# Routing attention and feed-forward: batch 2's feed-forward by seven products too, behind the attention

## The chip, the cores and the metric

The kernel runs on one core of one Trainium2 chip. The metric is the device time of a run in microseconds; three runs of the kernel before gave 957.65, 957.71 and 958.09 us, so the median is 957.71 us. PE is TensorE (matmuls), PEld its weight loads, DVE is VectorE, ACT is ScalarE, POOL is GpSimd, SP is SyncE, which only issues DMAs here.

## The reference

Inputs: `q`, `k`, `v` of 4 batches x 8 heads x 768 tokens x 64, and 16 centroids per head; `w_in` 512 x 2048, `w_out` 2048 x 512, `alpha` 2048, both weight matrices in double precision.

```python
q_assign = np.argmax(np.einsum('bhsd,hcd->bhsc', q_n, c_n), axis=-1)
k_assign = np.argmax(np.einsum('bhsd,hcd->bhsc', k_n, c_n), axis=-1)
mask = q_assign[:, :, :, None] == k_assign[:, :, None, :]
scores = np.where(mask, scale * np.matmul(q, k.transpose(0, 1, 3, 2)), -1000000000.0)
attn = softmax(scores)
x = np.matmul(attn, v)                 # then (B,H,S,D) -> (B*S, H*D) = 3072 x 512
h = x @ w_in
g = np.maximum(h, 0.0) + alpha * np.minimum(h, 0.0)
out = g @ w_out                        # 3072 x 512
```

A query attends only to keys of the same cluster. The feed-forward of one batch is 768 x 512 by 512 x 2048 and 768 x 2048 by 2048 x 512, in fp32.

## The kernel before, in words

**Attention.** Two heads make a pair; there are 16 pairs, four to a batch. Pairs 0 to 9 are taken in halves of 384 queries, each half in three steps: scores for all six chunks of 128 keys, exp on ScalarE, a mask on VectorE (`mask`, L795; from pair 4 on), sums for the denominators (`add_up`, `turn`, `rows_sums`), and the weighing of v on TensorE (`weigh`, L878). Pairs 10 to 15 are sorted by cluster first, so that each chunk of keys needs only two or three chunks of queries; a sorted pair is taken whole, in three steps (`add_near`, L819; `weigh_near`, L921; `normalise_near`, L937). The sort (`order_features` to `order_clusters`, L562 to L643) computes ranks on VectorE; then GpSimd scatters tokens into `scratch` by 24 indirect DMAs (`order_scatter`, L655) from two `stage` tiles that SP loads (`order_stage`, L645), and SP loads the sorted pair (`order_load`, L669). `ORDERS` (L1330) holds the step at which each sorted pair's sort begins. After a sorted pair, 12 indirect DMAs put the result back in token order (`put_back`, L970), SP fetches it (`fetch_back`, L977), and VectorE turns it into x (`turn_back`, L989).

The order of all work is written out by hand: one loop over 78 steps, each of five slots; a counter, `tick()`, runs with the slots, and `later(n, piece)` puts a piece n ticks on. In the first step of a half or pair (L1467 to L1494) come: scores of three chunks, the inverse of the prior pair's denominators (`invert`, L860), its weighing, three masks, its normalising, and scores of the other three chunks. The totals that `invert` reads are a TensorE matmul (`total`, L850), issued a few slots after the row sums, in the prior pair's own last slots.

**Feed-forward.** Regular feed-forward of half a batch (`ffn_pieces`, L1010) is 28 *pieces*: 16 hidden pieces (four matmuls of 384 columns, a copy on ScalarE, the slope on VectorE) and 12 finals (four matmuls of 512 columns; two finals fill one bank). They lie in a queue, `ffn`, and the loop takes some in each slot, so that TensorE has work while the attention waits. When a half of a batch's attention is done, `feed_block` (L1387) puts its 28 pieces in the queue; they are spread evenly over the slots of the next block of steps, and `kept` (L1396) says how many are left over at the block's end. Blocks, named here by letters, with their start and end in the profiled execution:

| block | steps | attention in it | pieces taken, before | us |
|---|---|---|---|---|
| A | 24 to 35 | pairs 4 to 7, first halves | 30 | 196.6 to 324.9 |
| B | 36 to 47 | pairs 4 to 7, second halves | 28 | 324.9 to 452.5 |
| C | 48 to 59 | sorted 10 and 11; 8 and 9, first halves | 26 | 452.5 to 571.5 |
| D | 60 to 65 | 8 and 9, second halves | 22 | 571.5 to 652.9 |
| E | 66 to 77 | sorted 12 to 15 | 24 | 652.9 to 761.9 |

What is left, 12 pieces, covers the last pair's way back (`while due`, L1536: two ticks for each piece). Then `last_pieces` (L1103) does batch 3 by seven products for eight (Strassen's scheme in Winograd's form): the x of the batch is split in four quarters, `w_in` and `w_out` likewise, sums of quarters are formed on VectorE (`sum_x` L1092, `w_in_sums` L1080, `g_sums` L1179, `w_out_sums` L1186), and seven products of quarters are added up in PSUM and on VectorE. First eight inner tiles x of `hidden` (L1197; six pieces of two matmuls of 384 columns and one late one), then three token tiles of `final` (L1253; seven products of eight matmuls of 256 columns). Sums of g are formed per inner tile, for all tokens at once, beside the hidden products.

Of the kernel before, what the change touches and what calls it, by code (L numbers as in the profile page):

```python
# [23 lines left out]
def kernel(  # L24
# [629 lines left out]

    def order_scatter(n, i, x):  # L655
        h, part = divmod(i, PARTS)
# [12 lines left out]
    def order_load(n):  # L669
        whole = scratch.pop(n)[0]  # L670
# [266 lines left out]
    def normalise_near(n):  # L937
# [20 lines left out]
        later(starts[1] + 2 + (HJ if dense else NJ), lambda: fetch_back(n, whole))  # L958
# [18 lines left out]
    def fetch_back(n, whole):  # L977

        b, hp = pairs[n]
        raw = inp.tile([P, 2, NJ, D], FP32, name="qk").rearrange("p h j d -> p (h j d)")  # L980
# [8 lines left out]
        def turn_back():  # L989
            for half in range(2):  # L990
                nc.vector.transpose(out=x_tile(b, half)[:, hp, :],
                                    in_=raw[:, half * HS:(half + 1) * HS])
        later(4 if n == NP - 1 else 9, turn_back)

# [12 lines left out]

    unfinished = [False]
# [61 lines left out]
    KH, NQ, HC = NCH // 2, NF // 2, DM // 2  # L1070
# [7 lines left out]
    by_pair, x_sums = {}, []  # L1078
# [13 lines left out]
    def sum_x(which):  # L1092
        x0, x1 = (xTs[B - 1, half] for half in range(2))
        if not x_sums:
            x_sums.extend(vpool.tile([P, 2, NJ, D], FP32, name="vt").rearrange(
                "p h j d -> p (h j d)").rearrange("p (c q) -> p c q", c=KH)
                for _ in range(3))
        T1, T2, T4 = x_sums
        B11, B21, B12, B22 = (x0[:, 0:KH], x0[:, KH:NCH], x1[:, 0:KH], x1[:, KH:NCH])
        for to, x, y in ((T1, B12, B11), (T2, B22, T1), (B12, B22, B12), (T4, B21, T2))[which]:  # L1100
            nc.vector.tensor_tensor(out=to, in0=x, in1=y, op=ALU.subtract)

    def last_pieces():  # L1103
        b = B - 1
        rows = out[b * S:(b + 1) * S, :].rearrange("(j p) n -> p j n", p=P)
        g, ys, s4, order = {}, [], [], []

        def places():

            whole = [e.rearrange("p h q -> p (h q)") for e in e_tiles]  # L1110
            whole += [inp.tile([P, 2, NJ, D], FP32, name="qk").rearrange(
                "p h j d -> p (h j d)") for _ in range(4)]
            single = [gpool.tile([P, HS], FP32, name="gT") for _ in range(NF // 2)]
            for x in range(NQ):
                for f in (x, NQ + x):
                    if whole:
                        t = whole.pop(0)
                        g[f] = [t[:, h * HS:(h + 1) * HS] for h in range(2)], t
                    else:
                        g[f] = [single.pop(0) for _ in range(2)], None  # L1120
            assert not whole
            s4.extend(single)
            more = [accp.tile([P, 2 * NX, Q], FP32, name="acc").rearrange("p x i -> p (x i)")
                    for _ in range(2)]
            more.append(vpool.tile([P, 2, NJ, D], FP32, name="vt").rearrange(
                "p h j d -> p (h j d)"))
            s4.extend(t[:, h * HS:(h + 1) * HS] for t in more for h in range(2))
            assert len(s4) >= NQ
# [13 lines left out]
        def slopes(f):  # L1142
            halves, both = g[f]
            for t in halves if both is None else [both]:
                nc.vector.scalar_tensor_tensor(out=t, in0=t, scalar=alpha[:, f:f + 1], in1=t,
                                               op0=ALU.mult, op1=ALU.max)
# [10 lines left out]
        def g_sum(x, m):  # L1157

            if m == "S4":
                return s4[x]  # L1160
            t = by_pair[x // 2].rearrange("p (x m q) -> p x m q", x=2, m=2)
            return t[:, x % 2, ("S1", "S2").index(m)]

        def g_form(m, x, t):
            r = slice(t * P, (t + 1) * P)
            if m in ("11", "12", "22", "S3"):
                f, half = {"11": (x, 0), "12": (NQ + x, 0), "22": (NQ + x, 1), "S3": (x, 1)}[m]
                return g[f][0][half][:, r]
            return g_sum(x, m)[:, r]
# [8 lines left out]

        def g_sums(x):  # L1179
            (t0, t1), (z0, z1) = g[x][0], g[NQ + x][0]  # L1180
            S1, S2, S4 = (g_sum(x, m) for m in ("S1", "S2", "S4"))
            for to, p, q, op in ((S1, t1, z1, ALU.add), (S2, S1, t0, ALU.subtract),
                                 (t1, t0, t1, ALU.subtract), (S4, z0, S2, ALU.subtract)):
                nc.vector.tensor_tensor(out=to, in0=p, in1=q, op=op)
# [12 lines left out]
        def hidden(x):  # L1197
# [3 lines left out]
            def product(to, m, rhs, start):  # L1201
                if start:
                    bank[to] = new_bank(to)[:, 0:HS]
                for cc in range(KH):
                    nc.tensor.matmul(out=bank[to], lhsT=w_in_form(m, x, cc),  # L1205
                                     rhs=rhs[:, cc, :], start=start and cc == 0,
# [3 lines left out]
            def x_of(half, kh):  # L1210
                return xTs[b, half][:, kh * KH:(kh + 1) * KH]

            def g_of(f, half):
                return g[f][0][half]

            def p1():
                if not g:
                    places()
                copy(g_of(f1, 0), product("a", "11", x_of(0, 0), True))

            def p5():
                copy(g_of(f2, 1), product("e", "S1", x_sums[0], True))
# [535 lines left out]
```

## Time and profile before

| | |
|---|---|
| median of three runs | 957.71 us |
| the profiled execution's own time | 958.22 us |
| its span, first to last instruction | 956.3 us |
| granted TensorE clock, mean | 0.997 |
| attention beside regular feed-forward, blocks A to E | 565.3 us |
| from there to the first of batch 3's products | 41.1 us |
| batch 3: hidden products, second products and the end | 73.8 and 79.5 us |

A profile shows how long each engine was busy and what it waited for. Idle time of an engine that is not the bottleneck costs nothing. In the tables by stretch the number in brackets is a count of instructions. TensorE records each fp32 matmul twice.

### The profile page before, as it was taken

The numbers are of one execution on the slowest core, as the hardware profiler recorded it, in microseconds if no ns is written. First come the engines' busy times: TensorE is split into PE (matmuls) and PEld (weight loads), VectorE is DVE, ScalarE is ACT, GpSimd is POOL, SyncE is SP. The second block draws the span as 40 slices with busy tenths as digits, with TensorE's granted clock in tenths as the row PEclk, the third lists the DMA queues.
The fourth block names the chain that finished last, engine by engine and source line by source line (L and its number), as shares of the span: only waits on it lengthen the run. The fifth ranks groups of instructions, "written<-read, shape, count | busy, mean of one in ns | idle before, by whom it ended". The sixth has DMA issues, their size and how long they took to land.

```text
span 956.3 us, 11347 instructions
## 1 busy us (share of the span) xinstructions
PE 929.1 (97%) x3995; PEld 496.8 (52%) x3995; DVE 669.4 (70%) x1235; ACT 251.5 (26%) x462; POOL 297.8 (31%) x333
## 2 busy tenths in 40 slices
PE   8999999999999999989999999999999999999997
PEld 5534444445454454444544545545455454556886
DVE  5797698799588697788894975556888536598100
ACT  5664544323032121220222212222122110221000
POOL 1433222210006365423277774640055440000000
PEclk9999999999999999999999999999999999999998
DMA  7433666047004444432842236441041011000000
GB/s 293 140 112 108 143 124 135 17 89 164 1 0 110 121 121 85 83 64 66 138 97 61 57 83 117 96 85 34 23 88 33 21 34 52 1 0 1 23 23 25
DMA packets 209664, 73.35 MB, mean 77 GB/s; under 512 B 194288, under 2 KB 198080, under 8 KB 209600
## 3 DMA queue, kind: packets, MB, share of 16 engines
q1 hardware_dynamic: 201840, 60.35, 28.5%
q0 software_dynamic: 6912, 11.81, 3.7%
q8 instruction: 33, 0.54, 0.2%
q10 hardware_dynamic: 848, 0.39, 0.2%
q14 instruction: 31, 0.25, 0.1%
HBM read 49.89 MB, written 22.28 MB: 75 GB/s over the span
## 4 chain that ended last, share of the span: by engine, by line
PE 77%; DVE 12%; issue 8%; POOL 2%; ACT 1%; DMA 0%; DVEq 0%; POOLq 0%; ACTq 0%
PE fps L1045 23%; PE fps L1027 17%; PE vps L901 7%; PE sps L765 6%; PE sps L1261 4%; PE sps L1205 4%; PE fps L765 2%; PE vps L1261 2%; PE vps L1205 2%; DVE acc L816 1%; PE fps L1261 1%; PE fps L1205 1%; DVE gT L1019 1%; DVE more L806 1%; PE vps L934 1%
## 5 line engine op out<-in xcount | busy, mean ns | idle before, releaser
L1027 PE MATMUL fps<-xT,w_in_sb 128*128 128x384 f32 x768 | 259.2, 491 | 0.0
L1045 PE MATMUL fps<-w_out_sb,gT 128*128 128x512 f32 x576 | 255.7, 596 | 1.1 <-DVE gT L1019 1.1
L663 POOL DMA_INDIRECT scratch<-stage,off x144 | 155.0, 1076 | 222.7 <-DMA stage<-in_v_dram 95.6
L1027 PEld LDWEIGHTS fps<-xT,w_in_sb 128*128 128x128 f32 x768 | 142.4, 190 | 103.6 <-issue 3.9
L1045 PEld LDWEIGHTS fps<-w_out_sb,gT 128*128 128x128 f32 x576 | 107.0, 190 | 129.0 <-issue 119.6
L972 POOL DMA_INDIRECT back<-rows,found x72 | 74.3, 1032 | 113.4 <-ACT rows L967 94.0
L1033 ACT COPY gT<-fps 128x384 f32<-128x384 f32 x96 | 46.0, 479 | 230.3 <-PE fps L1027 230.3
L1019 DVE SCALAR_TENSOR_TENSOR gT<-gT,alpha 128x384 f32<-128x384 f32 x96 | 61.5, 649 | 49.7 <-ACT gT L1033 49.5
L765 PE MATMUL sps<-qkT 64*128 64x384 f32 (+1 forms) x480 | 89.2, 490 | 0.0
L806 DVE SCALAR_TENSOR_TENSOR more<-aq,key,more 128x384 f32<-128x384 bf16 (+1 forms) x120 | 65.0, 598 | 19.3 <-ACT more L786 15.7
L786 ACT ACTIVATE E<-sps 128x768 f32<-128x768 f32 (+1 forms) x78 | 58.3, 796 | 62.5 <-PE sps L774 38.4
L765 PEld LDWEIGHTS sps<-qkT 64*128 64x128 f32 x480 | 42.8, 186 | 41.4 <-issue 14.4
L806 DVE SCALAR_TENSOR_TENSOR E<-aq,key,E 128x384 f32<-128x384 bf16 (+1 forms) x96 | 51.6, 595 | 17.7 <-ACT E L786 15.4
L901 PE MATMUL vps<-E,vt 128*64 128x384 f32 x316 | 58.6, 495 | 1.5 <-DVE xT L1003 1.5
L271 POOL TENSOR_TENSOR w_in_sb<-w_in_sb,power 128x512 f32<-128x512 f32 x16 | 26.9, 1683 | 67.8 <-DVE w_in_sb L268 67.8
L816 DVE TENSOR_TENSOR acc<-acc,E 128x768 f32<-128x768 f32 x37 | 35.2, 952 | 14.7 <-ACT E L786 13.6
L786 ACT ACTIVATE more<-sps 128x768 f32<-128x768 f32 (+1 forms) x42 | 31.4, 783 | 40.6 <-PE sps L765 40.0
L271 POOL TENSOR_TENSOR w_out_sb<-w_out_sb,power 128x512 f32<-128x512 f32 x16 | 22.6, 1412 | 56.0 <-DVE w_out_sb L268 56.0
L1051 ACT COPY y<-fps 128x512 f32<-128x512 f32 x18 | 10.6, 586 | 105.7 <-PE fps L1045 105.7
L1053 DVE TENSOR_TENSOR y<-y,fps 128x512 f32<-128x512 f32 x24 | 16.4, 683 | 29.8 <-PE fps L1045 29.8
L901 PEld LDWEIGHTS vps<-E,vt 128*64 128x64 f32 x316 | 20.1, 136 | 29.3 <-issue 26.8
L765 PE MATMUL fps<-qkT 64*128 64x384 f32 x144 | 31.8, 509 | 0.0
(281 smaller groups left out, 1106.1 us busy)
## 6 DMA issues: line engine op xcount, KB each, us to landing
raw<-in_moe_w_in_dram SPq DMA_DIRECT2D x16, 512.0 KB, 5.8
raw<-in_moe_w_out_dram SPq DMA_DIRECT2D x16, 512.0 KB, 4.3
out_dram<-y SPq DMA_DIRECT2D x21, 256.0 KB, 2.1
qk<-in_q_dram SPq DMA_DIRECT2D x48, 96.0 KB, 4.0
qk<-in_k_dram SPq DMA_DIRECT2D x48, 96.0 KB, 3.7
qk<-scratch SPq DMA_DIRECT2D x48, 96.0 KB, 3.4
w_in_kept<-w_in_sb SPq DMA_DIRECT2D x8, 512.0 KB, 4.7
vt<-in_v_dram SPq DMA_DIRECT2D x10, 384.0 KB, 4.3
```

The costliest lines, as they stand in the source:

```text
L271: nc.gpsimd.tensor_tensor(out=dst, in0=dst, in1=power[0].bitcast(FP32), op=ALU.mult)
L663: nc.gpsimd.indirect_dma_start(out=scratch[n][1][h * NX + xx], out_offset=bass.IndirectOffsetOnAxis(ap=ranks[n][:, xx, h:h + 1], axis=0), ...
L765: nc.tensor.matmul(out=bank(ps, h, m), lhsT=qkT[r:r + D, S + c * P:S + (c + 1) * P], rhs=qkT[r:r + D, tokens], start=True, stop=not early_ ...
L786: nc.scalar.activation(out=E[:, :, 0:m], in_=ps[:, :, 0:m], func=AF.Exp, scale=SCALE)
L806: nc.vector.scalar_tensor_tensor(out=e, in0=of, scalar=keys[n][:, NJ + c, h:h + 1], in1=e, op0=ALU.is_equal, op1=ALU.mult)
L901: nc.tensor.matmul(out=po[r:r + D, 0:HS], lhsT=vts[n][:, h, c, :], rhs=e[:, h, :], start=(c == 0), stop=(c == NJ - 1))
L972: nc.gpsimd.indirect_dma_start(out=to[i], out_offset=bass.IndirectOffsetOnAxis(ap=place[:, h, j:j + 1], axis=0), in_=rows[j // HJ][:, j % ...
L1019: nc.vector.scalar_tensor_tensor(out=gs[f], in0=gs[f], scalar=alpha[:, f:f + 1], in1=gs[f], op0=ALU.mult, op1=ALU.max)
L1027: nc.tensor.matmul(out=ps[:, 0:HS], lhsT=w_in_sb[:, c, f * P:(f + 1) * P], rhs=xTs[b, half][:, c, :], start=(c == 0), stop=(c == NCH - 1))
L1045: nc.tensor.matmul(out=ps[:, 0:DM], lhsT=gs[f][:, i * P:(i + 1) * P], rhs=w_out_sb[:, f, :], start=on and f == f0, stop=off and f == f0 + ...
L1205: nc.tensor.matmul(out=bank[to], lhsT=w_in_form(m, x, cc), rhs=rhs[:, cc, :], start=start and cc == 0, stop=cc == KH - 1, skip_group_check ...
L1261: nc.tensor.matmul(out=bank[to], lhsT=g_form(m, x, t), rhs=w_out_form(n, x), start=start and x == 0, stop=x == NQ - 1, skip_group_check=no ...
```

## The change

Regular feed-forward is now made only for batches 0 and 1. Batches 2 and 3 both go by seven products, after the attention: first the hidden products of batch 2, then of batch 3, then the second products of batch 2's three token tiles and batch 3's three. The regular pieces that are left are spread anew (`kept`). To find room, sums of g are formed per token tile: after each product of `final` that used a sum, the same sum for the next token tile is formed in its place. Batch 3's x lies in four E tiles, and its pairs 12 to 14 are fetched back after the last step. The matmul of totals moves from the pair's last slots to the next pair's first step, behind its first scores. Two scatters may go in a slot of the first step. Sorts begin at other steps, and the features of a sort come one step after the load instead of two.

```diff
-        later(starts[1] + 2 + (HJ if dense else NJ), lambda: fetch_back(n, whole))
+        backs[n] = whole
+        if pairs[n][0] < B - 1:
+            later(starts[1] + 2 + NJ, lambda: fetch_back(n))
+        elif dense:
+            for i in range(NCH):
+                later((1, 3, 5, starts[1] + 2 + HJ)[i],
+                      lambda i=i: fetch_back(NP - NCH + i))
...
+    def x_quarter(b, half, kh):
+
+        if b < B - 1:
+            return x_tile(b, half)[:, kh * KH:(kh + 1) * KH]
+        return e_tiles[2 * half + kh]
...
+    def sum_x(b):
+        B11, B21, B12, B22 = (x_quarter(b, half, kh) for half in range(2) for kh in range(2))
...
+        for c in range(KH):
+            for to, x, y in ((T1[c], B12[:, c], B11[:, c]), (T2[c], B22[:, c], T1[c]),
+                             (T4[c], B21[:, c], T2[c])):
+                nc.vector.tensor_tensor(out=to, in0=x, in1=y, op=ALU.subtract)
+        nc.vector.tensor_tensor(out=B12, in0=B22, in1=B12, op=ALU.subtract)
...
+        def g_sums(b, t, m):
             r = slice(t * P, (t + 1) * P)
+            for x in range(NQ):
+                t0, t1, z0, z1 = (g_tile(b, k, x)[:, r] for k in ("11", "21", "12", "22"))
+                p, q, op = {"S1": (t1, z1, ALU.add), "S2": (g_sum("S1", x), t0, ALU.subtract),
+                            "S3": (t0, t1, ALU.subtract),
+                            "S4": (z0, g_sum("S2", x), ALU.subtract)}[m]
+                nc.vector.tensor_tensor(out=g_sum(m, x), in0=p, in1=q, op=op)
...
                 late.append(p4)
-                if x % 2 == 0 and x:
-                    g_sums(x - 2)
-                    w_out_sums(x - 2)
-                    if x // 2 + 1 < NQ // 2:
+                if b == B - 2:
+                    if x in (2, 4):
                         w_in_sums(x // 2 + 1)
                 elif x > 1:
-                    g_sums(x - 2)
                     w_out_sums(x - 2)
+                    if x == NQ - 1:
+                        g_sums(B - 2, 0, "S1")
...
+                if m in ("S1", "S2", "S3", "S4") and k + 1 < 2 * HJ:
+                    g_sums(B - 2 + (k + 1) // HJ, (k + 1) % HJ, m)
...
-            def store(i, c0, c1):
-                nc.sync.dma_start(out=rows[:, i, c0:c1], in_=ys[i][:, c0:c1])
+            def store(i, *halves):
+                for c0 in halves:
+                    nc.sync.dma_start(out=rows[b][:, i * HJ + t, c0:c0 + HC],
+                                      in_=(y1 if i else y0)(c0))
...
         pieces = []
-        for x in range(NQ):
-            pieces += hidden(x)
-        pieces.append(room_for_y)
-        for t in range(HJ):
-            pieces += final(t)
+        for b in (B - 2, B - 1):
+            for x in range(NQ):
+                pieces += hidden(b, x)
+        pieces.append(second_products)
+        for k in range(2 * HJ):
+            pieces += final(k)
         return pieces
...
-    ORDERS = [26, 30, 34, 38, 41, 51]
+    ORDERS = [26, 29, 35, 38, 41, 50]
...
-                at(t + 2, 2 + i, lambda n=n, i=i: order_features(n, i))
-            at(t + 3, FIRST + 1, lambda n=n: order_sims(n))
+                at(t + 1, FIRST + i, lambda n=n, i=i: order_features(n, i))
+            at(t + 2, 2, lambda n=n: order_sims(n))
...
-            for i, p in ((5, 0), (7, 1)):
-                ffn[i] = lambda piece=ffn[i], p=p: (piece(), w_in_sums(p))
+            sums = [lambda: sum_x(WHOLE - 1), lambda: w_in_sums(0), lambda: w_in_sums(1)]
+            for i, also in enumerate(sums):
+                ffn[i] = lambda piece=ffn[i], also=also: (piece(), also())
             ffn.extend(last_pieces())
-            return
-        ffn.extend(ffn_pieces(*feeds[u]))
+        elif feeds[u][0] < WHOLE - 1:
+            ffn.extend(ffn_pieces(*feeds[u]))
...
-        return {NS: 12, begun_at[-2]: 8, begun_at[-3]: 2}.get(block_end(u), 0)
+        return dict(zip(begun_at[-5:], (7, 12, 19, 14, 6))).get(block_end(u), 0)
...
                 score(n, half, range(0, NJ // 2), alone=NJ // 2 - 1)
+            total(prior[0])
             tick()
...
-                todo += [lambda: None] * 4 + [lambda n=n: total(n)]
+                todo += [lambda: None] * 5
...
-            while sorting:
+            room = 1 + (s == 0)
+            while sorting and room:
                 scatters, piece = sorting.popleft()
                 piece()
-                if scatters:
-                    break
+                room -= scatters
...
+    late_pieces = len(ffn) - kept(NS - 1)
     while due:
         tick()
-        if due:
-            tick()
-        feed(1)
-    sum_x(slice(0, 4))
+        feed(1 if unfinished[0] or len(ffn) > late_pieces else 3)
+    sum_x(B - 1)
```

## The prediction

> **What bounds the kernel now.** I read the page first, then the busy time of each engine by stretch, then the chain of waits, then the instructions of VectorE and GpSimd in order of time. "Block" and "piece" are meant as in the section on the kernel.
>
> ```profile
> span 956.3 us, 11347 instructions
> ...
> PE 929.1 (97%) x3995; PEld 496.8 (52%) x3995; DVE 669.4 (70%) x1235; ACT 251.5 (26%) x462; POOL 297.8 (31%) x333
> ...
> PE   8999999999999999989999999999999999999997
> ...
> DVE  5797698799588697788894975556888536598100
> ```
>
> TensorE is busy 97% of the span with no weak slice but the ends: it sets the time, and only 27 us could be won by filling its gaps. VectorE has 70% over all, but eight or nine tenths in many slices of the attention. The busy time by block (columns: stretch, its length, PE, PEld, DVE, ACT, POOL, granted clock, DMA share, GB/s):
>
> ```profile
> 196.60:324.90 128.30, 126.24 (x469) 61.18 (x468) 98.27 (x178) 27.94 (x53) 22.70 (x31) 1.00 0.33 75
> 324.90:452.50 127.60, 123.05 (x473) 60.62 (x472) 106.44 (x191) 28.25 (x53) 57.42 (x61) 1.00 0.41 93
> 452.50:571.50 119.00, 114.96 (x475) 58.79 (x474) 95.09 (x174) 28.93 (x57) 75.86 (x79) 1.00 0.42 87
> 571.50:652.90 81.40, 81.40 (x287) 41.50 (x286) 45.41 (x76) 17.39 (x34) 38.80 (x44) 1.00 0.51 99
> 652.90:761.90 109.00, 107.14 (x443) 55.41 (x442) 84.52 (x151) 27.32 (x55) 32.80 (x33) 1.00 0.17 35
> 761.90:803.00 41.10, 41.10 (x144) 21.32 (x144) 18.73 (x39) 4.11 (x9) 15.54 (x16) 1.00 0.18 40
> 803.00:876.80 73.80, 72.85 (x228) 42.51 (x227) 53.26 (x108) 14.86 (x31) 0.00 (x0) 1.00 0.02 8
> 876.80:956.30 79.50, 72.57 (x337) 63.53 (x335) 13.42 (x32) 4.96 (x13) 0.00 (x0) 0.97 0.06 21
> ```
>
> The first five rows are blocks A to E (565.3 us). TensorE stands still for 12.5 us of them, VectorE for 135.6 us. In A to E TensorE is full only because feed-forward pieces are laid between the attention's steps. The last two rows are batch 3's feed-forward by seven products: VectorE has room there.
>
> What a column costs on TensorE, from the chain that ended last (start, us, what; every fp32 matmul leaves two records):
>
> ```profile
> 304.19 17.16 PE fps L1045 x40
> 586.89 12.90 PE fps L1027 x40
> ...
> 824.03 2.58 PE sps L1205 x8
> ...
> 894.11 10.36 PE sps L1261 x48
> ```
>
> Per record 429 ns (512 columns), 322 (384), 322 (384, products), 216 (256, products): 0.84 ns a column everywhere. So seven eighths of the columns is seven eighths of the time.
>
> [...] In the blocks above the granted clock is 1.00 and no gap of TensorE is over 1.9 us[...]. [...] The trace has 558 ns for 384 and 422 for 256[...] (the nearest row, a 128x128 add at L545, took 0.29 us).
>
> **The change part by part.**
>
> 1. *TensorE's saving.* A batch of regular feed-forward is 2 x (64 matmuls of 384 columns at 0.645 + 48 of 512 at 0.858) = 165 us; by seven products 112 x 0.645 + 168 x 0.432 = 145 us. Saved: 20.5 us, certain.
>
> 2. *Fewer pieces beside the attention.* From the feeding rule with the new `kept`: 23 pieces in A (30 before), 23 in B (28), 22 in C (26 before, 21 plus one to finish a pair of finals), 4 in D (22), 8 in E (24), and 6 after. What the attention itself takes is block minus pieces: L1027 and L1045 have, in A, 43.42 us for 16 hidden pieces and 49.20 for 14 finals, so 2.71 and 3.51 us each; L1019 has 0.61 us of VectorE per hidden piece, L1053 0.68 per second final. Own times of the attention: PE 33.6, 37.4, 36.3, 16.1, 31.7; DVE 85.1, 94.8, 84.2, 35.9, 75.1.
>    - A: 15 hidden, 8 final: PE 33.6 + 40.7 + 28.1 = 102.4; DVE 85.1 + 9.2 + 2.0 = 96.3
>    - B: 11 and 12: PE 37.4 + 29.8 + 42.1 = 109.3; DVE 94.8 + 6.7 + 2.0 = 103.5
>    - C: 14 and 8: PE 36.3 + 37.9 + 28.1 = 102.3; DVE 84.2 + 8.5 + 2.0 = 94.7
>    - D: 4 finals: PE 30.1; DVE 35.9
>    - E: 8 hidden: PE 53.4; DVE 75.1 + 4.9 - 2.1 (two turn_backs go to the tail) = 77.9
>
>    VectorE has 408 us to do and TensorE 398. In D and E VectorE is the bound; in A to C the two are level. The larger of the two, block by block, is 427.8 us: the floor.
>
> 3. *What is lost above the floor.* How near VectorE comes to 100% when all waits for it is what decides. In the sorted pair from 707.0 on it runs from 707.6 to 732.5 with hardly a gap, and then:
>
> ```profile
> 729.93 1.00 DVE L991 STREAM_TRANSPOSE xT<-qk 128x384 f32<-128x384 f32 x2
> 730.85 0.59 DVE L869 RECIPROCAL inverses<-mps 64x24 f32<-64x24 f32 x2
> 731.48 1.04 DVE L876 STREAM_TRANSPOSE rd<-inverses 128x384 f32<-128x384 f32 x2
> 734.99 0.50 DVE L806 SCALAR_TENSOR_TENSOR more<-aq,key,more 128x256 f32<-128x256 bf16 x1 [2.47 <-ACT more L786]
> ```
>
>    The mask waits for exp, exp for scores that TensorE makes only after the pair's totals and a piece queued behind them. The moved `total` takes this away: scores go first, and behind the waiting total stand only the weighing and the second scores (4 + 2.3 us), which VectorE covers by the inverses and six masks (1.05 + 3.3 us) or waits about 1 us for. I take 95% in D and E: 37.8 + 82.0 = 119.8. In A to C the work isn't spread evenly over windows of three steps: the one from 478.0 had 28.9 us of DVE against 9 of TensorE's own and gets the argmax of pair 15 as well (5.5 us), while its neighbours have too much TensorE work. Window by window the larger of PE and DVE/0.97 sums to 107 + 113 + 110 = 330 us; block by block it was 314. Work can slip a little over a window's edge, so I take the middle, 322. Attention: 442 us, bounds 428 and 455.
>
> 4. *Behind the attention.* The last weighing 4.0 + 6 finals of 3.51 = 25 us (41.1 before). VectorE's inverses, sums of batch 2's x (4 x 0.95) and first sums of w_in (8 x 0.69), 13 us, lie beside it; without that cover they would cost these 13. Hidden products of two batches: 73.8, as before, + 72.2 = 146. Second products: 2 x 72.6. After the last matmul 6.9, unchanged. The round trip of the last pair (12 scatters, the fetch at tick 14, its turn at 18) has ticks of 3.9 us (three products of 1.29) where it had 1.7: better covered than before, when VectorE waited 4.1 us for it.
>
> 5. *Costed at nothing.* Sums of g: from 4 x 0.56 per inner tile to 32 x 0.291 = 9.3 us per token tile; with 1.3 of adding that is 10.6 us of VectorE beside 24.2 of TensorE, each sum needed some 20 us after its input is free. 24 half stores on SP of 0.4 us: nobody waits. The sums of w_out in batch 3's turn only, 1.7 us beside 9 of TensorE. Orders moved by a step: the same instructions on SP, POOL and VectorE, earlier; but features now one step after the load instead of two, some 13 us against 6 of issue and 4 of landing.
>
> Sum: 196.6 (unchanged) + 442 + 25 + 146 + 145.2 + 6.9 = 961.7 us of span, against 956.3. The profiled execution took 958.2, 1.9 more than its span; the median of the runs is 0.5 under that. So 963.1; **963 us**. It breaks even where the attention takes 436.6.
>
> **The rivals.**
>
> *The lag is absorbed; faster.* With scores ahead of totals TensorE has work while VectorE catches up, so busy windows borrow from idle ones and the attention takes 430, near its floor: 951 us. For it: in the window from 196.6 both engines stand at 94% or more at once. Against: TensorE can't pass a total before VectorE has ended the pair, so the borrowing is a few us per pair. It decides once VectorE and TensorE lose under 9 us over the floor. 27%.
>
> *GpSimd becomes the bound.* Each indirect DMA holds its queue 1.26 us:
>
> ```profile
> 508.98 0.96 POOL L972 DMA_INDIRECT back<-rows,found  x1 [0.30 <-issue]
> 510.25 0.96 POOL L663 DMA_INDIRECT scratch<-stage,off  x1 [0.30 <-issue]
> ```
>
>    C has 24 put_backs and some 56 scatters: 80 x 1.26 + 14 copies of about 0.5 = 108 us, in a block that shrinks from 119 to about 107. If POOL ends it 10 us late, SP, whose stage loads wait for scatters, issues pair 12's loads late; they have 19 us before VectorE needs them in a block D of 38, of which issue and landing take 12. Price 3 to 10 us: 971. Against: scatters depend only on stage loads and may run ahead of the steps. 13%.
>
> [...] up to 8 us, 970. 5%.
>
> *Forecast*, VectorE the bound and 440 to 450 us of attention: 55%, own range 958 to 971. That TensorE's products aren't fewer can't be: the count is in the loops.
>
> **How the numbers follow.** A difference of 0.2% (1.9 us) is about what a measurement of this kernel can tell from none. The forecast gives 2% faster, 7% same, 46% slower; the first rival 24% faster and 3% same; the others 18% slower. Together 26, 10 and 64%. The range takes the first rival's time in and the other two: 950 to 976.
>
> **What would show it.** Right: PE busy near 908 us and its share down to 94%; TensorE idle 40 to 50 us in the attention, most of it in D and E, waits ending on VectorE; last products from about 664 to 954. Wrong: attention under 437 us, or waits in it that end on POOL, SP or DMA; a clock under 1.00 before the last slice; gaps in the products behind VectorE's sums.

## The result, and the profile after

The changed kernel takes 983.88 us (median of 4 runs, 982.34 to 985.25), the kernel before beside it 957.90 us: the ratio is 1.0268, 95% interval 1.0248 to 1.0288. It is 26 us slower. The forecast was 963, "slower", with a range to 976: the side was right, the size was missed by 21 us, which is more than the range allowed.

Eleven of the later runs fell on chips where the kernel before itself took 977 to 1014 us, with waits, of ScalarE and VectorE above all, that the profile puts to no instruction and that it shows in none of the other runs; their ratios are told, but nothing below is built on them.

The page of the changed kernel (profiled execution 982.34 us):

```profile
span 980.6 us, 11912 instructions
...
PE 922.3 (94%) x4107; PEld 524.7 (54%) x4107; DVE 717.9 (73%) x1417; ACT 252.9 (26%) x468; POOL 299.9 (31%) x333
...
PE   8999999999999999998999766789999999999997
...
DVE  5797789799888799899882999974566456644430
...
PEclk9999999999999999999999898889999999999999
```

TensorE now has a hole in slices 23 to 26, 540 to 640 us, and in slice 23 and slices 25 to 27 the granted clock falls to eight tenths. VectorE has a hole too, a 2 in slice 22, just ahead of TensorE's: for most of a slice of 24.5 us the supposed bound stood still. The busy time by block (columns as before: stretch, length, PE, PEld, DVE, ACT, POOL, granted clock, DMA share, GB/s):

```profile
196.60:301.10 104.50, 103.49 (x415) 51.06 (x414) 97.79 (x182) 27.08 (x51) 29.69 (x39) 1.00 0.44 100
301.10:412.30 111.20, 109.53 (x429) 52.71 (x428) 101.15 (x181) 25.55 (x48) 69.46 (x74) 1.00 0.55 117
412.30:521.80 109.50, 102.64 (x442) 52.87 (x441) 94.30 (x172) 26.98 (x53) 70.63 (x72) 1.00 0.38 84
521.80:570.30 48.50, 35.64 (x142) 15.56 (x141) 33.17 (x55) 11.35 (x21) 27.66 (x29) 0.89 0.64 112
570.30:655.40 85.10, 62.42 (x314) 34.74 (x314) 78.13 (x141) 23.75 (x48) 32.03 (x31) 0.89 0.23 42
655.40:682.80 27.40, 27.36 (x85) 13.04 (x86) 13.63 (x23) 0.48 (x1) 7.21 (x8) 0.91 0.26 56
682.80:828.60 145.80, 144.84 (x458) 84.62 (x456) 81.21 (x155) 30.57 (x64) 10.05 (x10) 1.00 0.03 8
828.60:980.60 152.00, 146.60 (x676) 128.36 (x676) 63.13 (x223) 9.42 (x25) 0.00 (x0) 0.99 0.06 22
```

Set beside the terms of the prediction's sum:

| term | predicted, us | measured, us | off |
|---|---|---|---|
| up to block A | 196.6 | 196.6 | 0 |
| A, B, C | 322 | 325.2 | +3.2 |
| D | 37.8 | 48.5 | +10.7 |
| E | 82.0 | 85.1 | +3.1 |
| behind the attention | 25 | 27.4 | +2.4 |
| hidden products | 146 | 145.8 | -0.2 |
| second products and the end | 152.1 | 152.0 | -0.1 |
| span | 961.7 | 980.6 | +18.9 |

The rest of the miss is that the median lies 1.5 us over the profiled execution, where the prediction set it 0.5 under.

So block D carries more than half of it. The chain of waits in D (start, us, what):

```profile
531.12 0.52 SPq L997
531.64 0.04 issue
531.68 3.00 DMA qk<-back
...
534.81 1.04 DVE xT L1004 x2
...
537.24 2.73 DVE more L810 x5
...
549.60 0.96 DVE part L847
550.56 0.14 issue
550.69 0.59 PE mps L860 x2
```

The chain runs from the fetch of sorted pair 11 (`fetch_back`) to its turn (`turn_back`, L1004 now), from there through the masks and sums of the next half, and only then back to TensorE. The same place in VectorE's own instructions, in order of time (in brackets the idle time before, and what ended it):

```profile
516.59 1.03 DVE L477 STREAM_TRANSPOSE aq<-every 128x384 bf16<-128x384 bf16 x2
534.81 1.04 DVE L1004 STREAM_TRANSPOSE xT<-qk 128x384 f32<-128x384 f32 x2 [17.19 <-DMA qk<-back]
```

VectorE stands still for 17.19 us, 13 of them in block D, for data that no attention step needs: x of batch 2 is read by the feed-forward, behind block E. All inverses, masks and sums of the next half are written behind it. TensorE meets it 16 us on, as 6.80 us of idleness before the totals at 550.69. And why the fetch is late, from GpSimd's instructions and SP's queue:

```profile
520.33 0.96 POOL L666 DMA_INDIRECT scratch<-stage,off  x1 [0.31 <-issue]
521.60 0.96 POOL L666 DMA_INDIRECT scratch<-stage,off  x1 [0.30 <-issue]
522.86 0.96 POOL L984 DMA_INDIRECT back<-rows,found  x1 [0.30 <-issue]
524.12 0.96 POOL L666 DMA_INDIRECT scratch<-stage,off  x1 [0.30 <-issue]
525.08 0.20 POOL L663 COPY stage<-number 64x4 int32<-64x4 int32 x1
525.56 0.98 POOL L666 DMA_INDIRECT scratch<-stage,off  x1 [0.28 <-POOL stage L663]
526.85 0.95 POOL L984 DMA_INDIRECT back<-rows,found  x1 [0.31 <-issue]
...
530.19 2.02 SPq L997 DMA_DIRECT2D qk<-back  x4
```

GpSimd is never idle here for more than 0.3 us: the last `put_back` of pair 11 (L984) stands in line among the scatters (L666) of pair 15, whose attention begins at 634.5. It starts at 526.85 and ends at 527.80, lands some 2.1 us later (the trace's figure for this kind), and SP issues the fetch at 530.19.

In the kernel before, scatters stand among the put_backs of pair 11 too, and yet its turn waits for nothing. Its first and last put_back and its turn there, and its first put_back in the changed kernel:

```profile
529.90 0.96 POOL L972 DMA_INDIRECT back<-rows,found  x1 [2.38 <-ACT rows L967]
...
558.93 1.60 POOL L972 DMA_INDIRECT back<-rows,found  x1 [0.30 <-issue]
...
572.18 1.03 DVE L991 STREAM_TRANSPOSE xT<-qk 128x384 f32<-128x384 f32 x2
```

```profile
496.55 0.96 POOL L984 DMA_INDIRECT back<-rows,found  x1 [0.30 <-ACT E L787]
```

The twelve put_backs begin within 29.0 us there and within 30.3 in the changed kernel. Two other things differ, counted from ScalarE's first copy of the pair's rows (529.14 there, 485.29 here). GpSimd's queue is already full, so that the first put_back starts 11.3 us after that copy instead of 0.8. And VectorE comes to the turn after 32.3 us instead of 43.0: the turn lies as many ticks behind the rows as before, and these ticks take less time now, with fewer pieces in them. The fetch was issued 10.2 us ahead of VectorE's coming; now it is issued 12.6 us behind it. Of this shift of 22.8 us, 12.1 come from the later issue and 10.7 from VectorE's being earlier.

The second new thing is in block E, in TensorE's instructions. First scores of a sorted pair, in the changed kernel and then in the kernel before:

```profile
590.28 2.50 PE L769 MATMUL sps<-qkT 64*128 64x256 f32 x8 [6.17 <-DVE mine L453]
612.83 2.50 PE L769 MATMUL sps<-qkT 64*128 64x256 f32 x8 [5.25 <-DVE qkT L703]
634.54 2.50 PE L769 MATMUL sps<-qkT 64*128 64x256 f32 x8 [6.00 <-DVE qkT L703]
```

```profile
680.22 1.35 PE L765 MATMUL sps<-qkT 64*128 64x256 f32 x8
```

The same eight records take 2.50 us after gaps of 5.25 to 6.17 us, at a granted clock of 0.50, and 1.35 us with no gap before them, at 1.00. For shorter gaps the last section has measurements that differ.

### The profile page after: what moved, and what is told of

Its sections match the earlier page's. It is cut to its first block, busy times and chain, and to the rows that moved or that the text cites. A ratio compares the mean times of both kernels' runs of the same rounds, so it can differ in the third digit from the quotient of the medians.

```text
span 980.6 us, 11912 instructions
## 1 busy us (share of the span) xinstructions
PE 922.3 (94%) x4107; PEld 524.7 (54%) x4107; DVE 717.9 (73%) x1417; ACT 252.9 (26%) x468; POOL 299.9 (31%) x333
## 4 chain that ended last, share of the span: by engine, by line
PE 76%; DVE 17%; DMA 2%; issue 2%; SPq 1%; ACT 1%; POOL 0%; DVEq 0%; ACTq 0%; POOLq 0%
PE fps L1070 15%; PE fps L1052 12%; PE sps L1326 8%; PE sps L1265 8%; PE vps L905 7%; PE sps L769 6%; PE vps L1326 4%; PE vps L1265 4%; PE fps L769 2%; PE fps L1326 2%; PE fps L1265 2%; DVE more L810 2%; DVE E L810 2%; DVE acc L820 1%; DVE acc L839 1%
## 5 line engine op out<-in xcount | busy, mean ns | idle before, releaser
L666 POOL DMA_INDIRECT scratch<-stage,off x144 | 159.8, 1110 | 142.1 <-DVE off L619 51.7
L1070 PE MATMUL fps<-w_out_sb,gT 128*128 128x512 f32 x384 | 173.6, 603 | 1.1 <-DVE gT L1044 1.1
L1052 PE MATMUL fps<-xT,w_in_sb 128*128 128x384 f32 x512 | 173.1, 490 | 0.0
L1052 PEld LDWEIGHTS fps<-xT,w_in_sb 128*128 128x128 f32 x512 | 94.8, 190 | 69.5 <-issue 3.0
L1070 PEld LDWEIGHTS fps<-w_out_sb,gT 128*128 128x128 f32 x384 | 71.5, 191 | 89.2 <-issue 81.7
L769 PE MATMUL sps<-qkT 64*128 64x384 f32 (+1 forms) x480 | 92.7, 506 | 23.4 <-DVE qkT L703 13.3
L984 POOL DMA_INDIRECT back<-rows,found x72 | 75.5, 1049 | 105.5 <-ACT rows L979 85.1
L1058 ACT COPY gT<-fps 128x384 f32<-128x384 f32 x64 | 30.7, 479 | 154.2 <-PE fps L1052 154.2
L1044 DVE SCALAR_TENSOR_TENSOR gT<-gT,alpha 128x384 f32<-128x384 f32 x64 | 41.1, 661 | 2.2 <-ACT gT L1058 2.2
L905 PEld LDWEIGHTS vps<-E,vt 128*64 128x64 f32 x316 | 20.1, 136 | 27.2 <-issue 24.4
L787 ACT ACTIVATE more<-fps 128x384 f32<-128x384 f32 x36 | 15.7, 491 | 58.0 <-PE fps L769 58.0
L905 PE MATMUL vps<-more,vt 128*64 128x384 f32 x164 | 30.5, 514 | 0.0
```

What stands on the lines that cost most here:

```text
L666: nc.gpsimd.indirect_dma_start(out=scratch[n][1][h * NX + xx], out_offset=bass.IndirectOffsetOnAxis(ap=ranks[n][:, xx, h:h + 1], axis=0), ...
L769: nc.tensor.matmul(out=bank(ps, h, m), lhsT=qkT[r:r + D, S + c * P:S + (c + 1) * P], rhs=qkT[r:r + D, tokens], start=True, stop=not early_ ...
L905: nc.tensor.matmul(out=po[r:r + D, 0:HS], lhsT=vts[n][:, h, c, :], rhs=e[:, h, :], start=(c == 0), stop=(c == NJ - 1))
L984: nc.gpsimd.indirect_dma_start(out=to[i], out_offset=bass.IndirectOffsetOnAxis(ap=place[:, h, j:j + 1], axis=0), in_=rows[j // HJ][:, j % ...
L1052: nc.tensor.matmul(out=ps[:, 0:HS], lhsT=w_in_sb[:, c, f * P:(f + 1) * P], rhs=xTs[b, half][:, c, :], start=(c == 0), stop=(c == NCH - 1))
L1070: nc.tensor.matmul(out=ps[:, 0:DM], lhsT=gs[f][:, i * P:(i + 1) * P], rhs=w_out_sb[:, f, :], start=on and f == f0, stop=off and f == f0 + ...
```

## The experiments

Two causes stand out, late put_backs and the clock, and a question: is D's loss the wait itself, or would VectorE be late there anyhow? Each run was taken beside the kernel before on the same chip. The changed kernel was not timed again beside them: what a run is said to gain on it is a difference of two times, and by the ratios to the kernel before the first two gains would be 9.5 and 12.5 us instead of 8.5 and 11.6.

**The turn of x eight ticks later.** Nothing else is moved: VectorE gets to pair 11's turn later, by when the fetch has landed.

```diff
-        later(4 if n == NP - 1 else 9, turn_back)
+        later(4 if n == NP - 1 else 17 if b < B - 1 else 9, turn_back)
```

> The changed kernel, but VectorE turns pairs 10 and 11 back 17 ticks after their fetch is issued instead of 9. Theory 1 (VectorE's 17.2 us wait for pair 11's fetch in block D is the lost time; GpSimd's late put_backs feed it): the wait goes to under 3 us, block D falls from 48.5 us to 38 to 40, the time to about 973 us. Theory 2 (VectorE's own work sets D, the wait lies in slack): D stays within 3 us of 48.5, time 981 to 984. Theory 3 (the lower TensorE clock in D sets it): D stays and its clock stays at 0.89.

Measured: 975.36 us, ratio 1.0169 [1.0152, 1.0186], so 8.5 us off the change. Block D by engine, and what VectorE waited for from there on (us in total, times, longest):

```profile
523.10:561.40 38.30, 31.85 (x141) 14.26 (x140) 33.33 (x55) 11.35 (x21) 29.79 (x29) 0.99 0.51 104
...
DVE xT L1004 <- DMA qk<-back: 0.3, 1, 0.3
```

D goes from 48.5 to 38.3 us with the same work in it, and the wait from 17.2 to 0.3 us. The clock in D is 0.99: its 0.89 in the changed kernel came with the wait and was no cause of its own. E and what follows up to the first product take 114.7 us against 112.5, so 2.2 us are given back; pair 12's first scores now have a gap of 5.14 us before them and take 2.51 us too.

**The scatters held back for three steps.** This is at the other end of the same path: the turn stays where it was, and no scatters (nor the loads of `stage` that feed them) are issued in steps 54 to 56, so that the put_backs pass ahead of them in GpSimd's queue.

```diff
-            room = 1 + (s == 0)
+            room = 0 if 54 <= u < 57 else 1 + (s == 0)
```

> The changed kernel, but no scatters of the sort are issued in steps 54 to 56, where the 12 put_backs of pair 11 are due; the 14 scatters that lay there come later. Theory 1 (put_backs are late because GpSimd's queue is full of scatters at 1.26 us each): the last put_back of pair 11 ends 10 us or more earlier than 527 us into the span, VectorE's wait of 17.2 us falls under 5, time 972 to 976 us. Rival (put_backs are late because SP's queue or the rows copy on ScalarE is late): the put_backs end where they did, time 981 to 984.

Measured: 972.25 us, ratio 1.0137 [1.0120, 1.0154], 11.6 us off the change. GpSimd's put_backs between 480 and 540 us, first and last start at the end of the line, in the changed kernel and here:

```profile
L984 POOL DMA_INDIRECT back<-rows,found x15: 954/959/2152, 479.9 to 526.8; - x15
```

```profile
L984 POOL DMA_INDIRECT back<-rows,found x15: 954/961/2158, 479.5 to 507.2; - x15
```

The last one starts 20 us earlier, the turn runs at 517.19 without waiting, and D takes 35.9 us. What VectorE does next:

```profile
517.19 0.99 DVE L1004 STREAM_TRANSPOSE xT<-qk 128x384 f32<-128x384 f32 x2
524.02 0.48 DVE L873 RECIPROCAL inverses<-mps 64x12 f32<-64x12 f32 x2 [5.84 <-PE mps L860]
```

It waits 5.84 us for the totals, which in the changed kernel TensorE made while VectorE waited for the fetch (at 523.93). So 5.8 of the 17.2 us would have been lost to TensorE anyway: a wait of 17.2 us was worth 12.6 us of D. The scatters that were held come after: block E has 36.5 us of GpSimd instead of 32.0, and VectorE waits for no DMA in it. What fills GpSimd's queue earlier (two scatters in a slot of the first step, or the sorts that begin earlier) was not told apart.

**The totals back at their old place.** The prediction rested on the moved `total`: scores go first, then the totals. Here this one part is undone.

```diff
             score(n, half, range(0, NJ // 2), alone=NJ // 2 - 1)
-            total(prior[0])
...
-                todo += [lambda: None] * 5
+                todo += [lambda: None] * 4 + [lambda n=n: total(n)]
...
-                todo += [lambda: None] * 3
+                todo += [lambda: None] * 2
+                todo.append(lambda n=n: total(n))
```

> The changed kernel, but with the matmul of totals in the pair's last slots again, ahead of the next pair's first scores. If the moved totals keep VectorE fed where it is the bound, as the prediction says (2.5 us of waiting taken away per pair), blocks D and E (6 pairs or halves) and the VectorE-heavy windows of A to C grow by 1 to 2.5 us each: 8 to 25 us slower than the changed kernel's 983.9, 992 to 1008. If the order of totals and scores makes no difference because VectorE's queue is full anyway: 982 to 986.

Measured: 1007.25 us, ratio 1.0509 [1.0480, 1.0538], 23.4 us over the change. The longest of VectorE's waits in its block D:

```profile
DVE xT L1004 <- DMA qk<-back: 18.0, 1, 18.0
DVE E L810 <- ACT E L790: 5.8, 1, 5.8
```

The first is the wait of the changed kernel; the second, a mask waiting for exp, is of the kind that the prediction showed with 2.47 us in the kernel before; here it lasts 5.8 us. In the changed kernel's D the mask's waits for exp come to 0.8 us. D takes 59.2 us instead of 48.5, E and what follows up to the first product 118.3 instead of 112.5, A to C 332.8 instead of 325.2. So the moved totals do what step 3 of the prediction said, and are worth 23 us here. The lower clock is in this sum: gaps of 6.08 to 7.10 us, and one of 14.18 in D, stand before the totals in D and E, and the granted clock is 0.80 and 0.82 there (0.89 in both in the changed kernel). How much of the 23 us is waiting and how much is the clock was not told apart.

The counterpart is the kernel before with only its totals moved, by the same edit the other way round.

> The kernel before with one part of the change alone: totals behind the next pair's first scores. In that kernel TensorE is full, and VectorE's wait of 2.47 us is in slack: what can be won are the gaps of TensorE that end on row sums, argmax or rows, 12.5 us in blocks A to E at most. Theory: 2 to 6 us faster, 952 to 956 us. If the order matters only where VectorE is the bound: 957 to 959.

> The same kernel again, for the same reason: the kernel before with totals behind the next pair's first scores. The order helps where TensorE waits for row sums too: 952 to 956 us. The order matters only where VectorE is the bound: 957 to 959.

Both runs fell on the chips named above: 1.0077 [1.0045, 1.0109] and 1.0042 [1.0004, 1.0080]. They show no gain; whether the order helps where TensorE is full stays open.

**The clock.** Sixteen unread matmuls of 128 columns are added before the first scores from step 60 on, into columns of PSUM that nobody reads. They are extra work on TensorE, in its gaps where it has some. Theory A of the expectation takes the low clock behind the gaps of 5.25 to 6.17 us (0.50, and 2.50 us for eight records instead of 1.35) for a cost of its own, beside the waiting.

```diff
+    def keep_busy():
+        for _ in range(16):
+            nc.tensor.matmul(out=held[0][:, HS:512], lhsT=ident, rhs=ident,
+                             start=True, stop=True)
...
+            if u >= 60:
+                keep_busy()
             tick()
             if u < NS:
                 score(n, half, range(0, NJ // 2), alone=NJ // 2 - 1)
```

> The changed kernel with 16 matmuls of 128 columns added ahead of the first scores of every half or pair from step 60 on (and before the last weighing), into columns of PSUM that nothing reads: 3.5 us of TensorE work each, in gaps of 4 to 7 us. Theory A[...]: the granted clock in D and E goes from 0.89 to 0.98 or more, the first scores of a sorted pair from 2.50 us for eight records to 1.35, and E falls from 85.1 to 79 to 83: time 977 to 982 us. Theory B (the slower clock is hidden behind VectorE, which is the bound): the clock rises, E stays within 1.5 us, time 983 to 985. Theory C: the clock doesn't rise.

Measured: 979.43 us, ratio 1.0221 [1.0204, 1.0238]: 4.5 us faster than the change, with more work. E and what follows to the first product take 107.5 us against 112.5:

```profile
569.90:652.50 82.60, 73.11 (x443) 47.97 (x443) 78.17 (x141) 23.75 (x48) 32.65 (x31) 0.96 0.27 45
652.50:677.40 24.90, 24.90 (x85) 11.80 (x86) 13.56 (x23) 0.48 (x1) 7.73 (x8) 1.00 0.29 63
```

The clock in E rises to 0.96, less than expected; three of the four first scores are at 1.35 to 1.38 us, one still at 2.51. C, up to the first scores of step 60, grew by 3.5 us, for TensorE has no gap there, and D fell by 3.7 with its gap shortened: together they are as before, and the gain is E's.

**Both at once.** If late put_backs and the clock are two causes, they should add.

> Both edits together: no scatters in steps 54 to 56, and 16 unread matmuls of 128 columns ahead of first scores from step 60 on. If late put_backs and the halved clock are two separate losses, their gains add: 983.9 - 11.6 - 4.5 = 967.8 us, 966 to 970. If one hides the other: 971 to 975. A granted clock of 0.99 or more either way.

That run and two repeats were among those set aside above (1.0443, 1.0502 and 1.0472). The expectations of these repeats, and last of the one that counts:

> The same kernel again, since the kernel before itself took 977 to 1008 us beside its first run. Both edits together: no scatters in steps 54 to 56, and 16 unread matmuls ahead of first scores from step 60 on. Two separate losses: 966 to 970 us. One hides the other: 971 to 975.

> Both edits together: no scatters in steps 54 to 56, and 16 unread matmuls of 128 columns ahead of first scores from step 60 on. If late put_backs and the halved clock are two separate losses, their gains add: 983.9 - 11.6 - 4.5 = 967.8 us, 966 to 970, which is the forecast of 963 plus 5. If one hides the other: 971 to 975.

> Both edits together: no scatters in steps 54 to 56, and 16 unread matmuls of 128 columns ahead of first scores from step 60 on. If late put_backs and the halved clock are two separate losses, their gains add: 983.9 - 11.6 - 4.5 = 967.8 us, 966 to 970, which is the forecast of 963 plus 5. If one hides the other: 971 to 975.

Measured: 972.28 us, 1.0135 [1.0117, 1.0153]: no better than the held scatters alone. A miss; the windows say why. First the held scatters alone (D; E; behind), then with the added matmuls:

```profile
521.50:557.40 35.90, 31.81 (x142) 14.26 (x141) 32.25 (x53) 11.35 (x21) 25.42 (x27) 1.00 0.52 106
557.40:644.90 87.50, 64.72 (x315) 35.80 (x315) 78.47 (x141) 23.95 (x48) 36.53 (x37) 0.85 0.33 60
644.90:672.20 27.30, 27.30 (x85) 12.97 (x86) 13.55 (x23) 0.48 (x1) 7.14 (x8) 0.91 0.26 56
```

```profile
527.70:567.00 39.30, 38.96 (x206) 21.76 (x205) 32.48 (x53) 10.77 (x20) 28.11 (x28) 1.00 0.62 121
567.00:649.50 82.50, 72.24 (x446) 47.57 (x448) 78.83 (x142) 23.85 (x48) 33.88 (x33) 0.98 0.26 49
649.50:673.90 24.40, 24.40 (x84) 11.40 (x81) 13.02 (x22) 0.48 (x1) 7.50 (x7) 1.00 0.29 64
```

E and the stretch behind it gain 7.9 us at a clock of 0.98 and 1.00 instead of 0.85 and 0.91. But D loses 3.4 us, and the last three steps of C 3.6: the held scatters leave TensorE no gap at steps 60 and 63, and the sixteen matmuls take 3.73 us at each. The last 2.6 us were lost before step 57, in windows that neither edit was meant to touch: 1.0 ahead of block A, and 1.7 in block B, where sixteen records of 384 columns, from 366.08 us on, took 7.10 us instead of 5.41. Why is open. A run with the added matmuls from step 66 on only was meant to confirm this:

> Scatters held, and the sixteen unread matmuls only from step 66 on (block E and its end), none at steps 60 and 63. Theory (the late round trip in D and the half clock in E are two costs that add; the run with both gained nothing over scatters held alone because TensorE had no gap at steps 60 and 63, so that there the unread matmuls cost their own 3 us each): D near 36 us as with scatters held alone, E near 82 and the stretch behind near 25, granted clock 0.99 or more, time 963 to 968 us. Rival (the clock costs nothing once the scatters are held, since VectorE sets E's pace anyway): E stays at 87 and the time at 971 to 974.

It fell on one of the chips set aside (1.0241 [1.0195, 1.0286], the kernel before at 979.84 there). So it is read from these windows, and not shown by a time, that the two causes add where the pieces are spread as in the change.

**The pieces spread otherwise.** In the table by block after the change, A to C last 325.2 us with 315.7 of TensorE; in D and E TensorE has room. Fewer pieces in A to C and more in E: 21, 21, 19, 7, 14 and 4 behind, instead of 23, 23, 22, 4, 8 and 6. (The expectations say 6 and 15 for D and E; the trace counts 7 and 14.)

```diff
-        return dict(zip(begun_at[-5:], (7, 12, 19, 14, 6))).get(block_end(u), 0)
+        return dict(zip(begun_at[-5:], (9, 16, 25, 19, 4))).get(block_end(u), 0)
```

> The changed kernel with the regular pieces spread otherwise: kept 9, 16, 25, 19, 4 instead of 7, 12, 19, 14, 6, so 21, 21, 19, 6 and 15 pieces in blocks A to E and 4 behind them (23, 23, 22, 4, 8 and 6 before). Theory 1 (A to C have more TensorE work than VectorE work, E has 25 us of TensorE to spare, so a piece moved to E is free): A to C go from 325 to 303 to 310 us, E stays within 4 us of 85 with its clock at 0.97 or more, the stretch behind goes from 27 to 20; the wait for pair 11's fetch remains: 953 to 962 us. Theory 2 (VectorE bounds A to C already, and pieces in E hold back scores): A to C stay over 316 and E grows by what is put in, 975 to 985.

> The same kernel again, for the same reason: pieces spread 21, 21, 19, 6, 15 over A to E and 4 behind them. Theory 1 (a piece moved from A, B or C to E is free): A to C 303 to 310 us, E within 4 us of 85, 953 to 962 us. Theory 2 (VectorE bounds A to C already, pieces in E hold back scores): 975 to 985.

Alone it was run only on the chips set aside (1.0333 [1.0216, 1.0450] and 1.0267 [1.0150, 1.0384]), so that its own share isn't known. With the scatters held as well, it was set aside three times (1.0100, 1.0087, 1.0090) and once, the last, not:

> The same spreading of pieces, and no scatters in steps 54 to 56. Theory 1: as respread, and without the wait for pair 11's fetch: 943 to 950 us, under the 957.7 of the kernel before. If the wait had become hidden by the spreading: the same as respread. Theory 2: 965 to 975.

> The same kernel again, for the same reason: pieces spread anew and no scatters in steps 54 to 56. Theory 1: 943 to 950 us. The wait for the fetch already hidden by the spreading: as the run with the spreading alone. Theory 2: 965 to 975.

> No scatters in steps 54 to 56, and the regular pieces spread 21, 21, 19, 6 and 15 over A to E with 4 behind (23, 23, 22, 4, 8 and 6 in the change). Theory 1 (A to C have more TensorE work than VectorE work and E has 25 us of TensorE to spare, so a piece moved to E is free): A to C 303 to 310 us instead of 325, E within 4 us of 85, 943 to 950 us. Theory 2 (VectorE bounds A to C already and pieces in E hold back scores): 965 to 975.

> No scatters in steps 54 to 56, and the regular pieces spread 21, 21, 19, 6 and 15 over A to E with 4 behind (23, 23, 22, 4, 8 and 6 in the change). Theory 1 (A to C have more TensorE work than VectorE work and E has 25 us of TensorE to spare, so a piece moved to E is free): A to C 303 to 310 us instead of 325, E within 4 us of 85, 943 to 950 us. Theory 2 (VectorE bounds A to C already and pieces in E hold back scores): 965 to 975.

Measured: 954.13 us (951.09 to 955.41), ratio 0.9955 [0.9938, 0.9972]: with these two edits of one line each the change is 0.4% faster than the kernel before on this chip, where on those set aside its ratios are 0.9 to 1.0% over 1. Over the held scatters alone (972.25) the spread is worth 18 us. A to C take 309.6 us, as hoped; the time is 4 us above what was expected. Two gaps of 3.77 and 4.58 us were left before first scores, and behind them the scores again took 2.5 us. So the added matmuls were put at just these two steps (72 and 75):

```diff
+            if u in (72, 75):
+                keep_busy()
```

> Pieces spread anew and no scatters in steps 54 to 56, as in the run that took 954.1 us, with the 16 unread matmuls ahead of the first scores of pairs 14 and 15 (steps 72 and 75) alone, where that run still has gaps of 3.8 and 4.6 us and first scores at 2.50 us. If the halved clock costs there as it did in the changed kernel: 1 to 3 us less, 951 to 953. If VectorE covers it: 954 to 956.

Measured: 950.44 us (949.07 to 952.28), ratio 0.9909 [0.9886, 0.9931], the best of all kernels here, taken on this one chip. Block E without and then with them, and the first scores of the last pair with them:

```profile
545.10:633.50 88.40, 79.86 (x362) 42.61 (x363) 79.13 (x142) 24.83 (x50) 36.01 (x37) 0.94 0.30 55
```

```profile
547.90:634.00 86.10, 84.54 (x436) 49.06 (x438) 80.14 (x146) 24.62 (x50) 38.59 (x39) 1.00 0.31 58
...
607.74 3.18 PE L886 MATMUL vps<-ident 128*128 128x128 f32 x27
612.06 1.35 PE L769 MATMUL sps<-qkT 64*128 64x256 f32 x8 [1.15 <-DVE qkT L703]
```

A gap of 4.58 us becomes 3.2 us of unread matmuls and 1.15 us of waiting; the scores are back at 1.35 us. E, the stretch behind it included, goes from 106.1 to 102.5 us.

## Why the prediction was wrong

*Step 1, the saving,* was right: hidden and second products came out within 0.2 us of their terms. Its own working gives 20.1 us (164.9 less 144.8), not 20.5.

*Step 2, the work,* was right: predicted in A to C were 314.0 us of TensorE and 294.5 of VectorE, measured are 315.7 and 293.2; in D and E 113.8 of VectorE against 111.3 (D alone 35.9 against 33.2). All counts of pieces came as predicted. TensorE's total was 922.3 instead of 908, and that is no added work: D and E have 98.1 us of it where 83.5 were predicted, at a granted clock of 0.89. Not all of it is the clock: with the scatters held, D has 31.8 us at 1.00 where 30.1 were predicted.

*Step 3, what is lost above the floor,* failed, in one term of it: "I take 95% in D and E". VectorE was busy for 68% of D and 92% of E. The 95% came from asking which waits of TensorE's making hold VectorE up. For E that was right once the clock is kept: 82.6 us with the added matmuls, 95% of it VectorE's, where 82.0 were predicted. In D the 38.3 us with the turn out of the way lie near the 37.8 by luck: VectorE had less to do there, and was busy for 87%. What was not asked is what else VectorE has in its queue. `turn_back` waits for a round trip through GpSimd and SP, and its 17.2 us hold up what is written behind it: the inverses that come next, whose totals TensorE made at 523.93, start at 535.77, behind the turn, and VectorE runs nothing from 517.62 to 534.81. Of the 10.7 us that D was over its term, this wait accounts for all: without it D took 35.9 or 38.3 us instead of 48.5. The middle of 322 us for A to C was 3.2 short.

*The moved totals* did take the stall away: without them the change stands at 1007 us, 23.4 higher, the clock's part included.

*Step 4, the tail,* was 2.4 us short. The last pair's totals came after a 4.47 us gap, and the clock behind them was 0.91; with that gap filled the same stretch took 24.9 us, as predicted. *Step 5* held: sums of g took 287 to 293 ns each (means by tile), where 0.291 us was reckoned, which is what the one 128x128 add at L545 took in the kernel before; and TensorE stood still for 5.4 of the last 152 us, all of it after its last matmul. One cost "at nothing" was not nothing: "orders moved by a step: the same instructions on SP, POOL and VectorE, earlier". It was worked out for the features' time to land, and not for what the scatters are queued ahead of on GpSimd, nor for a turn that keeps its distance in ticks while the ticks get shorter.

*The rivals.* The second, GpSimd as the bound (13%), had the engine right and the block, C into D. It put POOL's end 10 us late and the price at 3 to 10 us; holding the scatters gave back 11.6. GpSimd was no bound of C, though: it had 62 indirect DMAs there instead of 80 and stood idle for 21 us, waiting for the loads of `stage`. The order in its queue did the harm, not its load. Its victim was wrong: not pair 12's loads but pair 11's way back, whose reader stands in VectorE's queue much earlier. The third (5%), a lower clock of TensorE in E, came true as well. Blocks A to E of the kernel before stand at 1.00 and don't show it, and the price, up to 8 us, was the author's estimate; filling the gaps gave 5.0 us in E and behind it in the changed kernel, and 7.9 with the scatters held. The sum was made as if these were alternatives to the forecast. They were additions to it: its 961.7 us of span, some 11 for the queue and some 5 for the clock are 978 of the 980.6. A range that let them add, by the prices set on them, would have reached 981. The first rival, the lag absorbed (951 us, 27%), names the time that the best version reaches, but not its parts: an attention of 436.2 us, not 430, and 16.4 us behind it, not 25. That took a cleared queue, another spread and a kept clock, which the change doesn't have.

## What to carry to other kernels

Before an engine is called the bound, go through its queue for instructions whose input makes a round trip through another busy queue; put them behind the time at which that queue delivers, or hold back what stands ahead in it and is needed later. A distance kept in steps of the program is no distance in time: when the change shortens the steps, ask again whether the trip still fits. And price a wait by what the engine would wait for next, not by its length (here 12.6 us for 17.2). When the bound moves from TensorE to another engine, its gaps come due: those of 5.25 to 6.17 us before first scores cost twice here, once as waiting and once as 2.50 us for eight records instead of 1.35, and fillers should lie only where such gaps are (a fill where there was none cost its own 3.7 us). Mishaps that act on different waits can add up: a range should let them, instead of weighing each against the forecast alone.

## What was not expected of the hardware

The length of a gap alone did not tell whether the clock behind it was lower: 3.77 us before the scores at 588.06 (pieces spread, scatters held) were followed by 2.51 us for the eight records, and 3.91 us before those at 570.30 in the changed kernel by 1.35. A gap of 2.60 us, behind the added matmuls, was followed by 2.51 us in the run with these alone (at 589.84) and by 1.35 us in the run with the scatters held too (at 586.98). Matmuls whose result nobody reads, 0.12 us a record, raised the granted clock in E from 0.89 to 0.96, and from 0.85 to 0.98 with the scatters held. And whole stretches of tens of us had GpSimd's queue full of indirect DMAs at 1.26 us apiece, so that an order of issue that moves no more bytes was worth 11.6 us.
